# Sums over keys in an attention and MLP kernel: squares turned and added on VectorE in place of a product with ones on TensorE

## The chip, the cores and the metric

The kernel runs on one core of a Trainium2 chip. The time is the device time of one execution in microseconds. A core has five engines with a queue each, which run their instructions in order and wait for one another through semaphores: TensorE (PE in the profile; its weight loads are PEld), VectorE (DVE), ScalarE (ACT), GpSimd (POOL) and SyncE (SP, which here issues the transfers). TensorE reads SBUF and writes PSUM, which is divided into 8 banks.

## The reference

Two blocks follow each other: attention with normalised queries and keys, and an MLP without bias.

```python
batch, n_heads, seq, head_dim = (8, 12, 448, 64)
q_n, k_n = (rmsnorm(q, g_q), rmsnorm(k, g_k))
scores = scale * np.matmul(q_n, k_n.transpose(0, 1, 3, 2))
scores = scores - np.max(scores, axis=-1, keepdims=True)
attn = np.exp(scores)
attn = attn / (np.sum(attn, axis=-1, keepdims=True) + 1e-09)
attn_out = np.matmul(attn, v)
x = attn_out.transpose(0, 2, 1, 3).reshape(B * S, H * D)   # 3584 x 768
h = x @ w_in                                               # 768 x 2048
g = h - np.tanh(h)
out = g @ w_out                                            # 2048 x 768
```

All data are float32. Scores are bounded by the gains, so that the kernel leaves the maximum out (`bounded_path`; the other branch, `general_path`, isn't taken with these inputs). The sum over keys, by which each query's values are divided, is what the change is about.

## The kernel before

**Pairs and slots.** Work on attention goes by pairs of heads: 8 batches of 6 pairs, 48 pairs `s` in all. A pair's scores are held with the keys on partitions: for each of the two heads and each chunk of 128 keys (three, and a last one of 64) a matmul (L499) writes 128 keys x 448 queries into a PSUM bank and ScalarE's exponential (L504) takes it to the tile `p` in SBUF. In the last chunk the queries' halves lie on the two halves of the partitions (`p_last`). The values are products with `p` as the moving operand (L539 for the last chunk, L551 for the others); each puts 32 columns of head dimension on 32 partitions, four beside each other in the array. `divide` (L585) multiplies them by the sums' reciprocals and writes the pair's `xT`, the MLP's input.

**The sum over keys.** From the 10th pair on (`add`, L513), VectorE first adds the four chunks elementwise: L521 and L522 add the three full ones into the tile `rows` (`early["sum"]`, 128 x 2 heads x 448 queries), `add_last` (L529) adds the last, in two halves. What is left is a sum over 128 partitions. `totals` (L557) gets it from TensorE: for each half of the queries and each head a matmul (L572) of `ones` (128 x 32) with 224 columns of `rows`, four matmuls beside each other, so that 32 partitions of the bank `dn` hold the same sum. The reciprocal (L577) takes it from there to `rs`.

**The MLP** is made from seven products per group, in place of eight (the order of the products is `ORDER`, 1, 5, 6, 2, 3, 7, 4): `hidden` for a batch's first layer and `project` for its second, both by `products` (L640). Hidden: 4 groups of 7 products of 6 matmuls; output: 3 groups of 7 products of 8 matmuls; in each 168 matmuls of 224 columns. They are a generator, `stream`. Three PSUM banks named `mm` serve them in turn; products 2, 3 and 7 add to the bank of 1, 5 and 6. So product 4 takes the bank that product 2 left, and the next group's product 1 that of product 3, its product 5 that of product 7. In `hidden`, product 2 is read by a tanh (ScalarE, L676) and a subtraction (VectorE, L677); 3, 7 and 4 are added up by VectorE first (L706; L702 and L703; L710), and their tanh and a subtraction on GpSimd (L677) come when the next product is out, from the list `late["todo"]`. Factors of the second layer come from `factors` (L687 and L688 on VectorE, L689 on GpSimd) and L721. L694 (hidden) and L757, L763 (output) are ScalarE's copies out of the banks.

**The order around the change** is written by hand: `bounded_path` issues each engine's instructions in program order (`manual_schedule`), so a call's place in `slot` is its place in every engine's queue. From pair 12 on each pair has one `slot(s)`: last scores of pair s+1, last values, totals, values and division of pair s, the other scores of s+1, loads; then 56 matmuls of the stream in steps of `run(gap / 2)`, which is 7 matmuls, with other work between the steps. After 7: `add(s + 1)` and the squares; after 14: the norms of pair s+2 (`norm_blocks`, with a power on GpSimd, L457); after 21: `add_last(s + 1)`; after 28: `scale_blocks` (L464); after 35 and 42: the turning of q and k by squares of 32x32 (L474, L478); then `run(gap)`, 14 more. Pairs before the 18th have their q and k turned by TensorE instead. Six slots make a batch: the first three carry `hidden`, the other three `project`; the first slot of a batch belongs to a pair divisible by 6. Another 5 banks (`sc`, function `sc_bank`) are handed out in turn to scores, `dn` and values.

Of the kernel before, what the change touches and what calls it, by code (L numbers as in the profile page):

```python
# [9 lines left out]
F32 = mybir.dt.float32  # L10
# [3 lines left out]
ALU = mybir.AluOpType  # L14
AX = mybir.AxisListType
# [122 lines left out]
def bounded_path(tc, ctx, q, k, v, moe_w_in, moe_w_out, out, g_col, ident, ones, half_ones, neg_half, early):  # L138
# [17 lines left out]
    nc = tc.nc  # L156
    B, H, S, D = q.shape
    DFF, DM = moe_w_out.shape
    P = 128
    CP = S // NCH  # L160
    NP = H // 2
# [7 lines left out]
    HS = S // 2  # L169
# [4 lines left out]
    BL = 32  # L174
# [23 lines left out]
    def bank_of(name):  # L198

        turns[name] += 1  # L200
        return banks[name][turns[name] % len(banks[name])]
# [189 lines left out]
    normed, turned, probs, sums, whole, xT, tt = {}, {}, {}, {}, {}, {}, {}  # L391

    def squares(s):
        squares_of(nc, early["sq"], early["n"], loaded["q", s], loaded["k", s])
# [33 lines left out]
    FIRST, NJ = 3, S // BL  # L428

    def by_blocks(s):  # L430
        return has(s) and steps[s][0] >= FIRST
# [51 lines left out]
    def sc_bank():  # L483
        return bank_of("sc")

    def scores(s, c):

        rr, kT, qT = turned[s]
        halves, keys, n = (1, P, S) if c < KF else (2, KR, HS)
        name, bufs = ("p", 2) if c < 2 else ("p_full", 1) if c < KF else ("p_last", 2)  # L490
        if c == 1:
            p = probs[s, 1] = probs[s, 0]
        else:
            p = probs[s, c] = pp.tile([P, 2, 2 if c < 2 else 1, n], F32, name=name, bufs=bufs)
        tiles = [sc_bank() for _ in range(2)]
        for i in range(halves):
            for h in range(2):
                r = slice(h * D, (h + 1) * D)
                nc.tensor.matmul(  # L499
                    tiles[h][i * keys : (i + 1) * keys, :n], lhsT=kT[r, c * P : c * P + keys],  # L500
                    rhs=qT[r, i * n : (i + 1) * n], start=True, stop=True,
                )
        for h in range(2):
            nc.scalar.activation(  # L504
                p[:, h, c if c < 2 else 0, :], tiles[h][:, :n], AF.Exp,
                scale=1.0 if rr is None else rr[:, 0, 2 * c + h : 2 * c + h + 1],
            )

    def full(s):

        return probs[s, 0][:, :, 0], probs[s, 1][:, :, 1], probs[s, 2][:, :, 0]
# [12 lines left out]
    def add_last(s):  # L524
        last = probs[s, KF][:, :, 0]
        for n in range(2 if sums[s] else 0):
            t = sums[s][0]
            part = t[n * KR : (n + 1) * KR, :, n * HS : (n + 1) * HS]
            nc.vector.tensor_tensor(out=part, in0=part, in1=last[n * KR : (n + 1) * KR], op=ALU.add)  # L529

    def last_values(s, av):

        v_nat, p = loaded["v", s], probs[s, KF]
        for n in range(2):
            keys = slice(n * KR, (n + 1) * KR)
            for m in range(2):
                for h in range(2):
                    r = (2 * m + h) * BL
                    nc.tensor.matmul(  # L539
                        av[n][r : r + BL, :HS], lhsT=v_nat[keys, h, KF, m * BL : (m + 1) * BL],  # L540
                        rhs=p[keys, h, 0], start=True, stop=False,
                    )

    def values(s, av):
        v_nat, p = loaded.pop(("v", s)), full(s)
        for n in range(2):
            for c in range(KF):
                for m in range(2):
                    for h in range(2):
                        r = (2 * m + h) * BL  # L550
                        nc.tensor.matmul(  # L551
                            av[n][r : r + BL, :HS], lhsT=v_nat[:, h, c, m * BL : (m + 1) * BL],
                            rhs=p[c][:, h, n * HS : (n + 1) * HS], start=False, stop=(c == KF - 1),
                        )
        return av

    def totals(s, dn):  # L557

        parts = [t[:, h, n * HS : (n + 1) * HS] for t in sums.get(s, ()) for n in range(2) for h in range(2)]
        parts = [(parts, [ones[:, :BL]] * 2)] if parts else []  # L560
        if not sums.pop(s):
            for p in full(s):
                parts.append(
                    ([p[:, h, n * HS : (n + 1) * HS] for n in range(2) for h in range(2)], [ones[:, :BL]] * 2)
                )
            last = probs[s, KF]
            parts.append(([last[:, h, 0] for _ in range(2) for h in range(2)], [half_ones[:, n] for n in range(2)]))
        for i, (moving, by) in enumerate(parts):
            for n in range(2):
                for h in range(2):  # L570
                    r = (2 * n + h) * BL
                    nc.tensor.matmul(  # L572
                        dn[r : r + BL, :HS], lhsT=by[n], rhs=moving[2 * n + h],
                        start=(i == 0), stop=(i == len(parts) - 1),
                    )
        rs = whole[s] = sp.tile([P, HS], F32, name="rs")
        nc.vector.reciprocal(rs, dn[:, :HS])  # L577

    def divide(s, av):
        b, hp = steps[s]  # L580
        rs = whole.pop(s)
        x = xT[b, hp] = xp.tile([P, S], F32, name="xT")
        for n in range(2):
            for m in range(2):
                nc.vector.tensor_tensor(  # L585
                    out=x[m * D : (m + 1) * D, n * HS : (n + 1) * HS],
                    in0=av[n][m * D : (m + 1) * D, :HS], in1=rs[n * D : (n + 1) * D], op=ALU.mult,
                )
        for c in range(NCH):
            del probs[s, c]  # L590
        if hp < HC:
            return
        c = hp - HC
        if c == 0:
            tt[b] = tp.tile([P, 3, HC, HS], F32, name="tt", bufs=1)
        eng = nc.vector if b == 0 and c == HC - 1 else nc.gpsimd
        x11, x12, x21, x22 = (xT[b, r][:, n : n + HS] for r in (c, hp) for n in (0, HS))
        t1, t2, t4 = (tt[b][:, i, c] for i in range(3))
        eng.tensor_tensor(out=t1, in0=x12, in1=x11, op=ALU.subtract)
        eng.tensor_tensor(out=t2, in0=x22, in1=t1, op=ALU.subtract)  # L600
        eng.tensor_tensor(out=x12, in0=x22, in1=x12, op=ALU.subtract)
        eng.tensor_tensor(out=t4, in0=x21, in1=t2, op=ALU.subtract)


    late = {}
# [223 lines left out]
    def run(ns):  # L829

        spent[1] += ns
        while spent[0] + 1.0 < spent[1]:
            took = next(stream, None)
            if took is None:
                return
            spent[0] += took
# [4 lines left out]
    def gap_ns(s):  # L841

        if s < 2 * NP:
            return H_NS / 12 if s % NP < 3 else 4 * S / ENGINE_NS * CD * CF / 12
        return (H_NS + O_NS) / (4 * NP)

    def has(s):
        return 0 <= s < NS

    def first_slot(s):  # L850
# [28 lines left out]
        if has(s):  # L879
            divide(s, av)  # L880
# [31 lines left out]
    def slot(s):  # L912

        gap = gap_ns(s)
        if has(s + 1):
            scores(s + 1, KF)
        dn = sc_bank()
        av = [sc_bank() for _ in range(2)]
        last_values(s, av)
        totals(s, dn)  # L920
        divide(s, values(s, av))
        if has(s + 1):
            for c in range(KF):
                scores(s + 1, c)
        if has(s + 2):
            load(s + 2, "v")
        if by_blocks(s + 3):
            load_blocks(s + 3)
        blocks = by_blocks(s + 2)
        run(gap / 2)  # L930
        if has(s + 1):
            add(s + 1)
        if blocks:
            square_blocks(s + 2)
        run(gap / 2)
        if blocks:
            norm_blocks(s + 2)
        elif has(s + 2):
            turn(s + 2, sc_bank(), sc_bank())
        ahead = has(s + 3) and not by_blocks(s + 3)  # L940
        if ahead:
            squares(s + 3)
        if has(s + 4) and not by_blocks(s + 4):
            load(s + 4, "qk")
        run(gap / 2)
        if has(s + 1):
            add_last(s + 1)
        run(gap / 2)
        if blocks:
            scale_blocks(s + 2)  # L950
        if ahead:
            norm(s + 3)
        run(gap / 2)
        if blocks:
            turn_blocks(s + 2, 0)
        run(gap / 2)
        if blocks:
            turn_blocks(s + 2, 1)
        if ahead:
            norm_q(s + 3)  # L960
        run(gap)

    load(0, "qk")
    load(1, "qk")
# [4 lines left out]
    for s in range(NP, NS):  # L969
        (early_slot if s < 2 * NP else slot)(s)  # L970
# [346 lines left out]
```

## Time and profile before

| | |
|---|---|
| median of 9 runs (lowest to highest) | 1430.39 us (1426.14 to 1435.13) |
| profiled execution: its time, its span | 1434.06 us, 1432.2 us |
| granted TensorE clock, mean | 0.989 |
| TensorE busy (matmuls; loads) | 1397.8 us; 1176.0 us |
| VectorE busy, instructions | 867.8 us, 1396 |
| ScalarE busy, instructions | 412.2 us, 790 |
| GpSimd busy | 530.6 us |
| products with ones, of `rows` (L572) | 304 records, 38 pairs |
| reciprocal (L577), from a bank `sc` | 42, 1556 ns each |

The span reaches from the first to the last instruction of one execution. Busy times are per engine and overlap. A float32 matmul leaves two records. An instruction's line is that of the kernel's source, and a tile is named without its buffer number. "Idle before" is time in which the engine waited in front of an instruction, and the name behind the arrow is what it waited for. The chain is the sequence of work that ended last, followed back from the end.

### The profile page before, as it was taken

Reading aid. Unit: us, or ns where it says so; the run is one execution under the profiler, and the core shown is the slowest. Engines: PE = TensorE matmul, PEld = TensorE weight load, DVE = VectorE, ACT = ScalarE, POOL = GpSimd, SP = SyncE. Lnnn points to the kernel's source line nnn. Section 1 sums busy time; section 2 is a strip of 40 time slices with the busy share of each in tenths; the row PEclk is TensorE's granted clock in tenths of the full one; section 3 lists DMA queues with packets and bytes.
Section 4 is the critical chain, followed back from the end, with each engine's and each line's share of the span. In section 5 each row is a group of like instructions: output and inputs, shape, how many; then the busy total and the mean of one; then the engine's idle time right before and its main releaser. Section 6 shows DMA issues by size and latency. Waiting matters only on the chain.

```text
span 1432.2 us, 25681 instructions
## 1 busy us (share of the span) xinstructions
PE 1397.8 (98%) x10032; PEld 1176.0 (82%) x10032; DVE 867.8 (61%) x1396; ACT 412.2 (29%) x790; POOL 530.6 (37%) x348
## 2 busy tenths in 40 slices
PE   6999899999999999999999999999999999999997
PEld 3568654478998899889889988988998898899997
DVE  3899878855644676556755567545765577522311
ACT  5765454223311322122221223113221222201100
POOL 4556555232521346214533145313462145401310
PEclk9999899999999999999999999999999999999999
DMA  8669787864566656666666656666567656365663
GB/s 182 162 193 245 235 243 199 217 201 139 168 170 155 167 164 168 173 162 168 179 151 178 171 153 180 170 158 164 164 170 173 166 165 180 119 179 173 187 195 90
DMA packets 355254, 249.73 MB, mean 174 GB/s; under 512 B 266484, under 2 KB 297396, under 8 KB 355124
## 3 DMA queue, kind: packets, MB, share of 16 engines
q1 hardware_dynamic: 355120, 248.00, 64.4%
q8 instruction: 81, 1.33, 0.4%
q14 instruction: 49, 0.40, 0.1%
q10 hardware_dynamic: 4, 0.00, 0.0%
HBM read 214.50 MB, written 33.42 MB: 173 GB/s over the span
## 4 chain that ended last, share of the span: by engine, by line
PE 91%; DVE 4%; DMA 2%; SPq 1%; ACT 1%; issue 1%; POOL 0%; ACTq 0%; DVEq 0%
PE mm L640 66%; PE sc L499 9%; PE sc L551 6%; PE mm L805 4%; PE sc L572 2%; PE sc L539 2%; DMA q_nat<-in_q_dram 1%; DMA w_raw<-in_moe_w_out_dram 1%; DVE w_out L82 1%; DMA gT<-in_moe_w_in_dram 1%; DVE rs L577 1%; PE mm L551 1%; PE sc L419 0%; DVE w_out L78 0%; DVE w_out L324 0%
## 5 line engine op out<-in xcount | busy, mean ns | idle before, releaser
L640 PE MATMUL mm<-xT,w_f 128*128 128x224 f32 x1392 | 275.6, 354 | 0.0
L640 PEld LDWEIGHTS mm<-xT,w_f 128*128 128x128 f32 x1392 | 262.1, 190 | 9.1 <-issue 7.8
L640 PE MATMUL mm<-gT,w_f 128*128 128x224 f32 x1344 | 263.0, 354 | 0.0
L640 PEld LDWEIGHTS mm<-gT,w_f 128*128 128x128 f32 x1344 | 252.8, 190 | 11.4 <-issue 9.1
L457 POOL TENSOR_TENSOR rr_mine<-rr_mine,neg_half 128x28 f32<-128x28 f32 x30 | 145.1, 4835 | 256.1 <-DVE rr_mine L456 256.1
L640 PE MATMUL mm<-tt,w_f 128*128 128x224 f32 x1044 | 208.7, 353 | 0.0
L640 PEld LDWEIGHTS mm<-tt,w_f 128*128 128x128 f32 x1044 | 197.0, 190 | 3.9 <-issue 3.9
L640 PE MATMUL mm<-tg,w_f 128*128 128x224 f32 x1008 | 197.7, 353 | 0.0
L677 POOL TENSOR_TENSOR gT<-s,th 128x448 f32<-128x448 f32 x96 | 122.6, 1284 | 200.5 <-ACT th L676 197.8
L640 PEld LDWEIGHTS mm<-tg,w_f 128*128 128x128 f32 x1008 | 190.6, 190 | 0.0
L499 PE MATMUL sc<-qT,kT 64*128 64x448 f32 (+1 forms) x960 | 167.5, 497 | 12.9 <-ACT p_last L504 9.5
L499 PEld LDWEIGHTS sc<-qT,kT 64*128 64x128 f32 (+1 forms) x960 | 70.7, 166 | 84.3 <-issue 49.0
L600 POOL TENSOR_TENSOR tt<-xT,tt 128x224 f32<-128x224 f32 x23 | 17.1, 744 | 232.2 <-DVE xT L585 232.1
L676 ACT ACTIVATE th<-s 128x448 f32<-128x448 f32 x96 | 55.6, 579 | 135.3 <-DVE s L706 58.2
L577 DVE RECIPROCAL rs<-sc 128x224 f32<-128x224 f32 x42 | 65.3, 1556 | 42.6 <-PE sc L572 42.4
L504 ACT ACTIVATE p<-sc 128x448 f32<-128x448 f32 x120 | 55.6, 550 | 109.2 <-PE sc L499 109.2
L135 POOL TENSOR_TENSOR rr<-rr,neg_half 112x8 f32<-112x8 f32 (+1 forms) x36 | 59.6, 1676 | 58.5 <-DVE rr L134 58.4
L551 PE MATMUL sc<-p,v_nat 128*32 128x224 f32 x1344 | 79.1, 353 | 0.0
L805 PE MATMUL mm<-gT,w_out 128*128 128x448 f32 x192 | 76.6, 556 | 0.0
L585 DVE TENSOR_TENSOR xT<-sc,rs 64x224 f32<-64x224 f32 x168 | 65.2, 388 | 9.7 <-PE sc L551 2.3
L464 DVE TENSOR_TENSOR qk_n<-qk_nat,rr_mine 128x896 f32<-128x896 f32 x30 | 46.4, 1547 | 39.3 <-POOL rr_mine L457 37.0
L805 PEld LDWEIGHTS mm<-gT,w_out 128*128 128x128 f32 x192 | 37.0, 197 | 37.7 <-issue 36.7
(136 smaller groups left out, 1635.4 us busy)
## 6 DMA issues: line engine op xcount, KB each, us to landing
w_f<-w_in SPq DMA_DIRECT2D x196, 384.0 KB, 3.2
w_f<-w_out SPq DMA_DIRECT2D x147, 512.0 KB, 4.1
w_raw<-in_moe_w_out_dram SPq DMA_DIRECT2D x16, 768.0 KB, 5.2
out_dram<-th SPq DMA_DIRECT2D x192, 56.0 KB, 1.9
w_in<-w_out SPq DMA_DIRECT2D x21, 384.0 KB, 6.3
qk_nat<-in_q_dram SPq DMA_DIRECT2D x120, 56.0 KB, 2.5
qk_nat<-in_k_dram SPq DMA_DIRECT2D x120, 56.0 KB, 2.4
gT<-in_moe_w_in_dram SPq DMA_DIRECT2D x32, 192.0 KB, 4.2
```

Source lines behind the costliest of these rows:

```text
L135: nc.gpsimd.tensor_tensor(out=r, in0=r, in1=neg_half[:rows], op=ALU.pow)
L457: nc.gpsimd.tensor_tensor(out=mine, in0=mine, in1=neg_half[:, :1].to_broadcast([P, 2 * NJ]), op=ALU.pow)
L464: nc.vector.tensor_tensor(out=n.rearrange("p i j d -> p (i j) d"), in0=loaded.pop(("qk", s)).rearrange("p i j d -> p (i j) d"), in1=rr[:, ...
L499: nc.tensor.matmul(tiles[h][i * keys : (i + 1) * keys, :n], lhsT=kT[r, c * P : c * P + keys], rhs=qT[r, i * n : (i + 1) * n], start=True, ...
L504: nc.scalar.activation(p[:, h, c if c < 2 else 0, :], tiles[h][:, :n], AF.Exp, scale=1.0 if rr is None else rr[:, 0, 2 * c + h : 2 * c + h ...
L551: nc.tensor.matmul(av[n][r : r + BL, :HS], lhsT=v_nat[:, h, c, m * BL : (m + 1) * BL], rhs=p[c][:, h, n * HS : (n + 1) * HS], start=False, ...
L577: nc.vector.reciprocal(rs, dn[:, :HS])
L585: nc.vector.tensor_tensor(out=x[m * D : (m + 1) * D, n * HS : (n + 1) * HS], in0=av[n][m * D : (m + 1) * D, :HS], in1=rs[n * D : (n + 1) * ...
L640: nc.tensor.matmul(bank[:, f * HS : (f + 1) * HS], lhsT=w[:, c * width + f, :], rhs=moving[p](c), start=(first and f == 0 and c == 0), sto ...
L676: nc.scalar.activation(th, h, AF.Tanh, bias=0.0, scale=1.0)
L677: eng.tensor_tensor(out=g[:, rows, cols], in0=h, in1=th, op=ALU.subtract)
L805: nc.tensor.matmul(bank[:, :S], lhsT=w_out_row(f, n // HC)[:, n % HC * P : (n % HC + 1) * P], rhs=g[:, f, :], start=(f == 0), stop=(f == C ...
```

## The change

For pairs from the 14th on (`s >= 13`, `FOLDED`), the four matmuls of `totals`, the bank `dn` and the reciprocal of 128 x 224 go. In their place `fold(s + 1)` stands in the slot before, right behind `add_last(s + 1)`: VectorE turns `rows` (128 x 896) by squares of 32x32, which puts 32 queries on partitions and 32 keys side by side, and adds up each 32; what is left, 4 partial sums for each query, lies on four groups of 32 partitions. Eight ScalarE copies of 32 x 14 bring the groups side by side (64 x 4 x 14: two heads of 32 partitions). `spread_sums(s + 1)` stands in the middle of the last `run(gap)`, which is split: VectorE adds the four, takes the reciprocal of 64 x 14, copies each 32 times and turns the squares back, so that `rs_T` (64 x 448) holds each query's reciprocal on all 32 partitions of its head. `divide` reads it with one index in place of the other.

```diff
+    FOLDED = 2 * NP + 1
+
+    def fold(s):
+
+        t = sums.pop(s)[0].rearrange("p h s -> p (h s)")
+        turned_sum = late["blocks"].tile([P, 2 * S], F32, name="sum_T")
+        nc.vector.transpose(out=turned_sum, in_=t)
+        part = late["blocks"].tile([P, 2 * NJ], F32, name="sum_32")
+        nc.vector.reduce_sum(part, turned_sum.rearrange("p (i k) -> p i k", k=BL), axis=AX.X)
+        acc = whole[s] = late["blocks"].tile([2 * BL, P // BL, NJ], F32, name="sum_g")
+        for h in range(2):
+            for g in range(P // BL):
+                nc.scalar.copy(
+                    out=acc[h * BL : (h + 1) * BL, g], in_=part[g * BL : (g + 1) * BL, h * NJ : (h + 1) * NJ]
+                )
+
+    def spread_sums(s):
+
+        acc = whole[s]
+        total = late["blocks"].tile([2 * BL, NJ], F32, name="sum_all")
+        nc.vector.reduce_sum(total, acc.rearrange("p g j -> p j g"), axis=AX.X)
+        nc.vector.reciprocal(total, total)
+        wide = late["blocks"].tile([2 * BL, NJ, BL], F32, name="sum_w")
+        nc.vector.tensor_copy(out=wide, in_=total[:, :, None].to_broadcast([2 * BL, NJ, BL]))
+        rs = whole[s] = late["blocks"].tile([2 * BL, S], F32, name="rs_T")
+        nc.vector.transpose(out=rs, in_=wide.rearrange("p j k -> p (j k)"))
...
@@ divide
-                    in0=av[n][m * D : (m + 1) * D, :HS], in1=rs[n * D : (n + 1) * D], op=ALU.mult,
+                    in0=av[n][m * D : (m + 1) * D, :HS],
+                    in1=rs[:, n * HS : (n + 1) * HS] if s >= FOLDED else rs[n * D : (n + 1) * D], op=ALU.mult,
...
@@ slot
-        dn = sc_bank()
+        dn = sc_bank() if s < FOLDED else None
         av = [sc_bank() for _ in range(2)]
         last_values(s, av)
-        totals(s, dn)
+        if s < FOLDED:
+            totals(s, dn)
...
+        folded = has(s + 1) and s + 1 >= FOLDED
         if has(s + 1):
             add_last(s + 1)
+        if folded:
+            fold(s + 1)
         run(gap / 2)
...
-        run(gap)
+        run(gap / 2)
+        if folded:
+            spread_sums(s + 1)
+        run(gap / 2)
```

## The prediction

> **What bounds the kernel now.** I read the page first, for the busiest engine and for what the chain of waits is made of.
>
> ```profile
> PE 1397.8 (98%) x10032; PEld 1176.0 (82%) x10032; DVE 867.8 (61%) x1396; ACT 412.2 (29%) x790; POOL 530.6 (37%) x348
> ...
> PE 91%; DVE 4%; DMA 2%; SPq 1%; ACT 1%; issue 1%; POOL 0%; ACTq 0%; DVEq 0%
> ```
>
> TensorE sets the end: busy is no proof, but 91% of the chain is. Then the chain in order of time, for the slot of pair 24, whose products with ones are the eight records of L572 (four matmuls), and for an early slot, where the totals stand elsewhere and L551 follows L539 directly.
>
> ```profile
> 103.19 2.41 PE sc L551 x48
> ```
> ```profile
> 631.75 0.54 PE sc L499 x8
> 632.29 0.54 PE sc L539 x16
> 632.83 0.52 PE sc L572 x8
> 633.34 2.27 PE sc L551 x48
> 635.61 2.60 PE sc L499 x12
> 638.21 21.39 PE mm L640 x112
> 659.59 0.54 PE sc L499 x8
> ```
>
> Columns: start, duration, engine and line. The slot lasts 27.84 us and no other engine stands in its chain. So a microsecond less on TensorE is a microsecond gained, and a microsecond that TensorE is made to wait is lost. What can make it wait is VectorE or ScalarE holding a PSUM bank. So I read the time line of both engines behind the place where `fold` will stand, in the same slot:
>
> ```profile
> 646.35 1.26 DVE L529 TENSOR_TENSOR rows<-rows,p_last 64x448 f32<-64x448 f32 x2
> 648.10 0.62 DVE L677 TENSOR_TENSOR gT<-mm,th 128x448 f32<-128x448 f32 x1 [0.49 <-ACT th L676]
> 650.80 1.09 DVE L464 TENSOR_TENSOR qk_n<-qk_nat,rr_mine 128x896 f32<-128x896 f32 x1 [2.08 <-POOL rr_mine L457]
> ```
> ```profile
> 647.52 0.54 ACT L676 ACTIVATE th<-mm 128x448 f32<-128x448 f32 x1 [5.43 <-PE mm L640]
> ```
> ```profile
> 651.67 2.27 PEld L640 LDWEIGHTS mm<-tt,w_f 128*128 128x128 f32 x12
> ```
>
> The tanh and the subtraction L677 read the bank of the second product; the fourth (moving `tt`, loads from 651.67) needs that bank. Today it is free at 648.72, 2.9 us early. Last, the groups of instructions, for prices:
>
> ```profile
> L577 DVE RECIPROCAL rs<-sc 128x224 f32<-128x224 f32 x42 | 65.3, 1556 | 42.6 <-PE sc L572 42.4
> L504 ACT ACTIVATE p_last<-sc 128x224 f32<-128x224 f32 x60 | 18.2, 355 | 104.9 <-PE sc L499 104.9
> L452 DVE TENSOR_REDUCE rr_mine<-qk_n 128x28 f32<-128x896 f32 x30 | 32.0, 1067 | 0.0
> L454 DVE COPY rr_other<-rr_mine 32x28 f32<-32x28 f32 x120 | 24.7, 206 | 3.5
> L474 DVE STREAM_TRANSPOSE qT<-qk_n 128x448 f32<-128x448 f32 x30 | 19.2, 638 | 0.5
> L1255 ACT ACTIVATE warm<-warm 1x1 f32<-1x1 f32 x1 | 0.2, 202 | 0.0
> ```
>
> **Removed: TensorE.** With L572 between, it and L551 take 0.52 + 2.27 us; without, L551 alone takes 2.41 (the early slot). Difference 0.38. The empty 0.36 us before L572's first load are not gained: in the early slots the same gap stands before L551. By starts the removal is 633.16 - 632.76 = 0.40 (first matmuls of L551 and L572). I take 0.375 for 35 pairs (13 to 47): **-13.1 us** (14.0 by starts).
>
> **Removed: VectorE and a bank.** The reciprocal of 1.56 us goes from each slot's start, with the bank `dn`. Neither was on the chain: the first scores that need a bank back from `divide` are the fourth and fifth tiles, in both orders of the banks, and `divide` now waits only for the values. I count 0 for this; what hides it is the score matmuls, which run 1 us before those tiles.
>
> **Added: VectorE.** In `fold` a transposition of 128x896: L474 takes 0.638 for 448 columns, and 448 more at 1.0 ns (an addition, L759, takes 0.392 for 224 and L698 0.612 for 448) make 1.09, say 1.10; and a reduction like L452, 1.07. In `spread_sums` two instructions of 14 results, some 0.2 (L455, 28 columns, has 0.188) and 0.25 (with 14 reciprocals at L577's 6.9 ns), a broadcast copy of 64x448 between 0.35 and 0.62 (the 448-wide L677 is the upper end), and a transposition like L474, 0.64: about 1.6. Together 3.8 for 1.56, some 80 us more over 35 slots: VectorE goes from 868 to about 948 us, 66%, and does not become the bound. The path of `spread_sums` itself has cover: emitted 7 matmuls (2.65 us) before the slot ends, with 2.4 us of scores, last values and first values behind it before `divide` can start: 5 us for 1.6. No DMA is added or moved, SP's queue is untouched, and GpSimd gets nothing new; it only gets its inputs later.
>
> **Added: ScalarE, the step that costs.** Eight copies of 32x14 stand in ScalarE's order behind the reduction, and everything emitted after them waits: that is the tanh above. I lay this out for pair 24's slot. L529 ends at 647.61; transposition to 648.74, reduction to 649.83, eight copies to 649.86 + C, tanh 0.54 more, L677 to 651.06 + C, some 0.05 for the release. The load wants the bank at 651.67, so TensorE waits **C - 0.56 us**.
>
> For C no row is the same. The smallest instruction on ScalarE took 0.202 us (L1255). Two of L504 take 0.61 together where one takes 0.355, an overlap of 0.10: eight at a pitch of 0.11 make 0.9. Without overlap they are 1.65; VectorE's four L454 (0.206 each, 0.76 together) are close to that. The copies resemble L504 by engine and L454 by size and by changing partitions, so I take the middle, C = 1.25 (0.9 to 1.7), and a wait of 0.7 us (0.3 to 1.1).
>
> Two pages of the Trainium skill price these copies. "VectorE: DVE Perf Modes", on the errata of operands in SBUF, speaks against the change: the fixed cost is paid per instruction, many small tiles pay it each, and tiles should have 512 elements or more; its 224 + 14 cycles at 1.2 GHz give 0.198 each, 1.6 in all, which would make the wait 1.0 and the forecast about 1423. "ScalarE: Activation LUTs", on what a table load costs, lets successive instructions overlap by 93 ns, which gives 0.93, a wait of 0.4 and about 1420. The smallest row agrees with the first's single price; whether they overlap no row shows.
>
> Now the six places in a batch. **First slot** (hidden layer starts; pairs 18, 24, 30, 36, 42 show the same times within 0.4 us): 5 x 0.7 = 3.5. For pair 12, L529 ends at 310.06 and L677 would end at 313.51 + C against a load near 314.7: 0.1. **Second slot**: the tanh of the third product (today 674.20) comes after the copies. Reduction done at 677.5; L702 and L703 follow to 678.6, and the bank they free is wanted by the next group's second product at 678.76. Tanh to 678.05 + C, GpSimd's subtraction to about 680.6, L687, L688, a transposition and L696 to some 685, wanted at 685.4. Margins of 0.1 and 0.4: I put 0.15 for each of five slots, 0.75; it grows one for one when C passes 1.7. **Third slot**: L696 done at 707.7, wanted at 708.0; the next tanh is due at 708.57, as the copies end: 0. **Fourth to sixth** (output layer): fold ends about 733.1, and the next ScalarE work, L763, comes at 734.08: 0.
>
> **Sum.** -13.1 + 3.5 + 0.1 + 0.75 = **-8.8 us**. The profiled execution took 1434.06 us around a span of 1432.2, 3.7 us over the median of the runs shown; the time outside the span does not change. 1425.3 for that execution is 1421.6 against the median 1430.39: 0.6% faster.
>
> **The rivals.**
>
> *All hidden*: the copies overlap and the bank is not late; -13.1 alone, 1417.3. For it: 2.9 us of slack today. Against: the reduction alone ends 2.2 us after L529, before any copy. 0.20.
>
> *Gain mostly eaten*: C near 1.9, or VectorE's added work stretched while GpSimd runs (L464 took 1.09 in one slot, 2.01 in the next), so that the second slots wait too: 5 x 1.3 + 0.7 + 5 x 0.6 = 10.2, net -2.9, 1427.5. For it: margins of 0.1 to 0.4 us there. 0.15, a third of it within the bound of no change. The change not doing what it says, TensorE meeting another wait where the products stood, would also end near 1430; against it, the values wait for nothing in today's chain. 0.03.
>
> *Slower*: ScalarE held by the copies. At 0.4 us a copy, C = 3.2: the first slots wait 5 x 2.65, pair 12 2.0, the second slots 5 x 1.65, together 23.5; net +10, 1440. It decides from C = 2.35, 0.29 us a copy. For it: the in-order queue, and that each copy changes partitions. Against: no ScalarE row of any size costs more than 0.20 fixed. 0.10.
>
> **How the numbers follow.** Forecast 0.52, all hidden 0.20, mostly eaten 0.15, no effect 0.03, slower 0.10. This kernel's measurement tells 0.2% (2.9 us) from no change. Faster: 0.52 + 0.20 + 0.10 = 0.82; within: 0.05 + 0.03 = 0.08; slower 0.10. The range: low 1415, all hidden with 0.40 us a pair and a microsecond or so of scatter between runs; high 1429, where the first slots wait 1.7 each and the second 0.8. Outside it are the slower case and part of no effect.
>
> **What would show it.** Right: 24 records of L572 on `rows` in place of 304, slots of the output layer 0.38 us shorter (27.46), the first slots of a batch longer than those, with a wait of a load at L640 for VectorE's L677 at the fourth product; eight ScalarE copies in 0.9 to 1.7 us; VectorE near 948 us. Wrong: waits of TensorE in second or third slots above 0.5 us, `divide` waiting for the transposition of `spread_sums`, or a gap beyond 0.36 us ahead of the values.

## The result and the profile after

| | before | changed |
|---|---|---|
| median | 1431.06 us (31 runs) | 1425.24 us (10 runs, 1422.94 to 1429.03) |
| ratio of the changed to before | | 0.9962, 95% interval 0.9952 to 0.9973 |
| profiled execution: time, span | 1434.06 us, 1432.2 us | 1420.67 us, 1418.9 us |
| span from pair 12's last values (first load of L539) to the end | 1137.95 us | 1131.55 us |

The change makes the kernel 0.4% faster, 5.8 us by the medians. The spans of the two profiled executions differ by 13.3 us, but 6.9 of these lie ahead of pair 12's last values, in code that the change leaves as it is: that place was reached between 287.4 and 294.3 us in the executions profiled for this study. The last row leaves this part out: 6.4 us. I use it below for all kernels.

The page after, engines and chain, answers to the first lines of before:

```profile
PE 1382.5 (97%) x9752; PEld 1162.6 (82%) x9752; DVE 928.2 (65%) x1571; ACT 467.1 (33%) x1070; POOL 524.5 (37%) x348
...
PE 87%; DVE 4%; DMA 3%; SPq 2%; ACT 2%; issue 1%; POOL 0%; ACTq 0%; DVEq 0%
```

TensorE has 280 records less, VectorE 60 us more work and ScalarE 55 more, and still TensorE is 87% of the chain. The chain in order of time over four slots (pairs 23 to 26; columns are start, duration, engine and line; L551 opens each slot's values):

```profile
596.47 2.41 PE sc L551 x48
...
623.93 2.41 PE sc L551 x48
626.34 2.60 PE sc L499 x12
628.94 4.75 PE mm L669 x24
...
652.67 2.41 PE sc L551 x48
...
680.13 2.41 PE sc L551 x48
```

From start to start a slot takes 27.46 us where it was 27.84, except for the first slot of the batch (from 623.93): 28.74. There the chain leaves the products (L669, line 640 before) after 24 records, which are twelve matmuls. The time lines of VectorE, ScalarE and the weight loads in that slot:

```profile
637.09 1.26 DVE L529 TENSOR_TENSOR rows<-rows,p_last 64x448 f32<-64x448 f32 x2
638.38 1.11 DVE L586 STREAM_TRANSPOSE sum_T<-rows 128x896 f32<-128x896 f32 x1
639.53 1.09 DVE L588 TENSOR_REDUCE sum<-sum_T 128x28 f32<-128x896 f32 x1
643.08 0.62 DVE L706 TENSOR_TENSOR gT<-mm,th 128x448 f32<-128x448 f32 x1 [2.46 <-ACT th L705]
```
```profile
640.71 1.77 ACT L592 COPY sum_g<-sum 32x14 f32<-32x14 f32 x8 [7.89 <-DVE sum L588]
642.50 0.54 ACT L705 ACTIVATE th<-mm 128x448 f32<-128x448 f32 x1
```
```profile
643.75 2.19 PEld L669 LDWEIGHTS mm<-tt,w_f 128*128 128x128 f32 x12 [1.35 <-DVE gT L706]
```

The tanh starts 0.02 us after the last copy, the subtraction (L706, before L677) ends at 643.70 and the fourth product's load starts at 643.75, after 1.35 us of waiting. Loads ahead of it end at 642.40, so this is where it was wanted. VectorE itself was idle for 2.46 us ahead of L706: it waited for ScalarE.

### The profile page after: what moved, and what is told of

Read it like the earlier page. It is cut to its first block, busy times and chain, and to the rows that moved or that the text cites. A ratio compares the mean times of both kernels' runs of the same rounds, so it can differ in the third digit from the quotient of the medians.

```text
span 1418.9 us, 25566 instructions
## 1 busy us (share of the span) xinstructions
PE 1382.5 (97%) x9752; PEld 1162.6 (82%) x9752; DVE 928.2 (65%) x1571; ACT 467.1 (33%) x1070; POOL 524.5 (37%) x348
## 4 chain that ended last, share of the span: by engine, by line
PE 87%; DVE 4%; DMA 3%; SPq 2%; ACT 2%; issue 1%; POOL 0%; ACTq 0%; DVEq 0%
PE mm L669 64%; PE sc L499 9%; PE sc L551 7%; PE mm L834 4%; PE sc L539 2%; DMA w_f<-w_in 1%; SPq L118 1%; SPq L265 1%; DMA w_raw<-in_moe_w_out_dram 1%; DVE w_out L82 1%; PE mm L551 1%; DMA gT<-in_moe_w_in_dram 1%; ACT sum_g L592 0%; DVE rs L577 0%; SPq L116 0%
## 5 line engine op out<-in xcount | busy, mean ns | idle before, releaser
L669 PE MATMUL mm<-xT,w_f 128*128 128x224 f32 x1392 | 275.6, 354 | 0.0
L669 PEld LDWEIGHTS mm<-xT,w_f 128*128 128x128 f32 x1392 | 262.1, 190 | 9.1 <-issue 7.2
L669 PE MATMUL mm<-gT,w_f 128*128 128x224 f32 x1344 | 263.0, 354 | 0.0
L669 PEld LDWEIGHTS mm<-gT,w_f 128*128 128x128 f32 x1344 | 252.8, 190 | 11.4 <-issue 6.5
L669 PE MATMUL mm<-tt,w_f 128*128 128x224 f32 x1044 | 209.4, 354 | 5.4 <-DVE gT L706 5.4
L669 PEld LDWEIGHTS mm<-tt,w_f 128*128 128x128 f32 x1044 | 196.5, 190 | 11.4 <-DVE gT L706 7.5
L669 PE MATMUL mm<-tg,w_f 128*128 128x224 f32 x1008 | 197.7, 352 | 0.0
L706 POOL TENSOR_TENSOR gT<-s,th 128x448 f32<-128x448 f32 x96 | 115.6, 1214 | 212.8 <-ACT th L705 212.7
L669 PEld LDWEIGHTS mm<-tg,w_f 128*128 128x128 f32 x1008 | 190.6, 190 | 0.0
L592 ACT COPY sum_g<-sum 32x14 f32<-32x14 f32 x280 | 56.3, 201 | 225.1 <-DVE sum L588 219.4
L613 DVE TENSOR_TENSOR xT<-sc,rs_T 64x224 f32<-64x224 f32 x140 | 54.4, 388 | 68.3 <-PE sc L551 66.4
L504 ACT ACTIVATE p<-sc 128x448 f32<-128x448 f32 x120 | 55.5, 548 | 97.8 <-PE sc L499 97.8
L551 PE MATMUL sc<-p,v_nat 128*32 128x224 f32 x1344 | 79.9, 355 | 0.0
L521 DVE TENSOR_TENSOR rows<-p 128x896 f32<-128x896 f32 x38 | 42.4, 1115 | 41.7 <-ACT p L504 41.7
```

What stands on the lines that cost most here:

```text
L504: nc.scalar.activation(p[:, h, c if c < 2 else 0, :], tiles[h][:, :n], AF.Exp, scale=1.0 if rr is None else rr[:, 0, 2 * c + h : 2 * c + h ...
L521: nc.vector.tensor_tensor(out=t, in0=p[0], in1=p[1], op=ALU.add)
L551: nc.tensor.matmul(av[n][r : r + BL, :HS], lhsT=v_nat[:, h, c, m * BL : (m + 1) * BL], rhs=p[c][:, h, n * HS : (n + 1) * HS], start=False, ...
L592: nc.scalar.copy(out=acc[h * BL : (h + 1) * BL, g], in_=part[g * BL : (g + 1) * BL, h * NJ : (h + 1) * NJ])
L613: nc.vector.tensor_tensor(out=x[m * D : (m + 1) * D, n * HS : (n + 1) * HS], in0=av[n][m * D : (m + 1) * D, :HS], in1=rs[:, n * HS : (n + ...
L669: nc.tensor.matmul(bank[:, f * HS : (f + 1) * HS], lhsT=w[:, c * width + f, :], rhs=moving[p](c), start=(first and f == 0 and c == 0), sto ...
```

## The experiments

Each kernel is the changed one with the edit shown. "From pair 12" is the span from pair 12's last values to the end (before 1137.95, changed 1131.55).

**1. The copies issued later.**

```diff
+    def gather(s):
+        part = late.pop("part")
         acc = whole[s] = late["blocks"].tile(...)
         ... the eight copies, out of fold ...
@@ slot, after 35 matmuls
         run(gap / 2)
+        if folded:
+            gather(s + 1)
         if blocks:
             turn_blocks(s + 2, 0)
```

> The same instructions as in the changed kernel; only the eight ScalarE copies are issued 14 matmuls later in each slot, ahead of the turning of q. Theory (13.1 us come from TensorE, and about 7 are lost because the first slots' tanh waits in ScalarE's queue behind copies that wait for VectorE): the tanh starts as the product ends, L706 ends about 641.3 in the slot where its bank is wanted at 642.4, no wait is left: 1418 us against 1431 before, ratio 0.991. Rival A (the loss comes from VectorE's own order, the transposition and the reduction standing ahead of the subtraction): first slots still 1.3 us longer, 1425. Rival B (the removed products are worth only 6 us and nothing is lost): 1425.

> The kernel with the copies issued 14 matmuls later once more, for a narrower interval: 1418 us, ratio 0.991 to 0.992.

Measured: 1418.52 against 1429.29 us, ratio 0.9922 (0.9895 to 0.9949), and 1415.02 against 1428.88 us in the longer comparison, 0.9901 (0.9882 to 0.9920). From pair 12: 1124.15 and 1123.90, 14 us less than before. The same instructions in the first slot of the batch, ScalarE and then VectorE:

```profile
641.98 0.54 ACT L710 ACTIVATE th<-mm 128x448 f32<-128x448 f32 x1 [5.43 <-PE mm L674]
644.43 1.77 ACT L597 COPY sum_g<-sum 32x14 f32<-32x14 f32 x8 [1.91 <-DVE sum L588]
```
```profile
643.26 1.09 DVE L588 TENSOR_REDUCE sum<-sum_T 128x28 f32<-128x896 f32 x1
644.26 0.61 DVE L711 TENSOR_TENSOR gT<-mm,th 128x448 f32<-128x448 f32 x1
```
```profile
646.13 2.27 PEld L674 LDWEIGHTS mm<-tt,w_f 128*128 128x128 f32 x12
```

The tanh is done by 642.52, the subtraction waits only for VectorE's reduction and ends at 644.87; the load at 646.13 has no idle time ahead of it. VectorE's order was unchanged, so rival A falls; the gain more than doubled, so rival B falls. This version beats both kernels.

**2. The copies on VectorE, at their old place.**

```diff
-                nc.scalar.copy(
+                nc.vector.tensor_copy(
```

> The eight copies are made by VectorE at the same place, behind the reduction. Theory: ScalarE is free, the tanh is done early, but the subtraction now waits behind eight copies of 0.19 us on VectorE: it ends about 642.7 where the bank is wanted at 642.4, a wait of 0.3 to 0.4 us in five slots: 1420 us, ratio 0.992. Rival A: the wait grows with what VectorE does there, to 2.8 us, 1433. Rival B: 1425, as the copies' engine does not matter.

Measured: 1461.48 us, ratio 1.0228 (1.0209 to 1.0246); from pair 12 1169.12, 31 us more than before. The theory and both rivals missed this. The first slot behaved as the theory said: from start to start 27.84, 0.38 of waiting. The second and third slots of the batch were the surprise, in the chain:

```profile
630.49 2.41 PE sc L551 x48
...
658.33 2.41 PE sc L551 x48
...
688.12 2.41 PE sc L551 x48
...
721.13 2.41 PE sc L551 x48
```

They take 29.79 and 33.01 us, 2.3 and 5.5 more than 27.46. In two of the five batches (pairs 31 and 43) the second slot takes 31.5, which experiment 5 comes back to. VectorE's time line gives the copies of the three slots, and the loads' time line the waits:

```profile
647.19 1.51 DVE L592 COPY sum_g<-sum 32x14 f32<-32x14 f32 x8
674.84 2.37 DVE L592 COPY sum_g<-sum 32x14 f32<-32x14 f32 x8
706.45 4.13 DVE L592 COPY sum_g<-sum 32x14 f32<-32x14 f32 x8
```
```profile
678.45 4.46 PEld L669 LDWEIGHTS mm<-tt,w_f 128*128 128x128 f32 x24 [2.41 <-DVE s L732]
711.29 6.14 PEld L669 LDWEIGHTS mm<-xT,w_f 128*128 128x128 f32 x24 [3.94 <-DVE s L725]
```

The evictions L732 and L725, queued behind the copies, release the banks that the next products want; these were the places for which the prediction had found margins of 0.1 and 0.3 us. And the copies are not the same everywhere: 0.19 us each in the first slot, 0.52 in the third, where GpSimd's 128x448 subtractions run from 706.85 to 710.16. That GpSimd is the cause was not tested. What else the third slot lost is told under experiment 5.

**3. The removal alone.**

```diff
     def fold(s):
+        sums.pop(s)
+        if s == FOLDED:
+            late["one"] = late["blocks"].tile([2 * BL, S], F32, name="rs_T")
+            nc.vector.memset(late["one"], 1.0)
+        whole[s] = late["one"]
+        return
...
     def spread_sums(s):
+        return
```

> The products with ones, the bank and the reciprocal are left out from the 14th pair on and nothing takes their place: the division reads a tile of ones, so the sums over keys of these pairs are not part of the result. Theory: all slots of the output layer and of the hidden layer are 27.46 us, 35 times 0.375 us less than before: 1418, ratio 0.991. Rival A: the same. Rival B: 1425, since that is all the products were worth.

Measured: 1416.44 us, ratio 0.9921 (0.9897 to 0.9944); from pair 12 1124.13, 13.8 less than before. All slots in its chain are 27.46 us from pair 17 on, where before has 27.84, and 28.39 for pairs 13 to 15, where before has 28.77. So TensorE's part of the change is worth 13.8 us, and the version of experiment 1, which does all the work, costs no more than this one, which does none of it.

**4. The added work alone.**

```diff
-        t = sums.pop(s)[0].rearrange("p h s -> p (h s)")
+        t = sums[s][0].rearrange("p h s -> p (h s)")
...
-        dn = sc_bank() if s < FOLDED else None
+        dn = sc_bank()
...
-        if s < FOLDED:
-            totals(s, dn)
+        totals(s, dn)
...  divide reads rs as before
```

> The products with ones and the reciprocal stay and are used; the turning, adding, the eight ScalarE copies and the spreading are done as in the changed kernel, their result unused. Theory: the added work alone costs five first slots 1.28 us each and pair 12's slot 0.6: 7.0 us, 1438 against 1431, ratio 1.005; VectorE also has the reciprocal, which ends before this. Rival A: the same 7. Rival B: 1431, nothing lost.

Measured: 1439.29 against 1429.29 us, ratio 1.0079 (1.0055 to 1.0102), so 10 us, and by the interval no less than 7.9; from pair 12 1146.23, 8.3 more than before. In the chain the first slots take 29.09 us (630.06 to 659.15) where 27.84 is the rule, the others from pair 17 on 27.84 to 27.88. That accounts for 1.25 in five slots, some 6.3 us. The slots of pairs 12 and 13 lost 2.2 together (from 288.59 to 348.38, 59.79 us, where before has 57.58) and not 0.6: besides a wait of 0.74 us for the subtraction in pair 12's slot, the score loads of pair 13's wait for the reciprocal.

```profile
321.79 0.29 PEld L499 LDWEIGHTS sc<-qT,kT 64*128 64x128 f32 x2 [1.23 <-DVE rs L577]
```

VectorE's queue was late there: one instruction (L404, the scaling of queries), just ahead, took 4.18 us where it took 0.77 at this place before, and the work of `spread_sums` followed. So "VectorE also has the reciprocal, which ends before this" was wrong in this one slot; the rest agrees with the theory.

**5. Every copy made twice.**

```diff
+        for twice in range(2):
             for h in range(2):
                 for g in range(P // BL):
                     nc.scalar.copy(
```

> All eight copies are made twice, so ScalarE is held 1.77 us longer in each of 34 slots. Theory (the wait is what ScalarE's queue holds back, less a margin): the five first slots wait 1.28 + 1.77 each, pair 12's 0.6 + 1.77, and the second slots, which today end within some 0.1 us of their margin, 1.7 each: 15.2 + 2.4 + 8.5 = 26 lost against 13.1 gained, 1444 us, ratio 1.009. Rival C (only the first slots are near their margin, the second ones are not): 1435.

Measured: 1449.68 us, ratio 1.0135 (1.0110 to 1.0159); from pair 12 1160.11, 22 more than before and 36 more than experiment 3, where 26 had been expected. The second slots lost 1.5 each (666.76 to 695.71, 28.95), where the theory had 1.7; rival C falls. TensorE waits there 0.76 us for ScalarE's own copy out of a bank (L724, L694 before) and 0.89 for the addition L726 (L696 before). The first slot of pair 24 took 31.95 us (634.81 to 666.76), 4.5 over the rule and not 3.05; the other four took 32.05 to 33.60. The loads' time line, and the group of the matmuls behind them (the number after the busy time is the mean in ns):

```profile
656.44 3.60 PEld L670 LDWEIGHTS mm<-tt,w_f 128*128 128x128 f32 x12 [3.16 <-DVE gT L707]
```
```profile
L670 PE MATMUL mm<-tt,w_f 128*128 128x224 f32 x12 | 3.9, 505 | 2.8 <-DVE gT L707 2.8
```

The wait of 3.16 us is the expected one. But the twelve loads behind it take 3.60 us where they take 2.19 in the changed kernel, and their matmuls 505 ns where 354 is the mean. The granted clock by stages says why (busy times of PE, PEld, DVE, ACT and POOL with their counts, then the clock, the share of the DMA engines and GB/s):

```profile
656.40:660.10 3.70, 3.65 (x12) 3.41 (x13) 3.11 (x5) 1.16 (x2) 1.43 (x2) 0.60 0.01 2
660.10:663.00 2.90, 2.90 (x17) 2.90 (x16) 2.45 (x5) 1.36 (x3) 0.95 (x2) 1.00 0.40 136
```

After 2.8 us without a matmul TensorE ran at 0.60 of its clock for 3.7 us: another 1.4 us lost. In experiment 2 the third slot shows the same: 3.94 us of waiting, and loads of 6.14 us where 24 take 4.54 in an undisturbed slot. Its second slot waited 2.41 us (2.1 without a matmul) and the 24 loads behind took 4.46: nothing lost. But the second slots are not alike. With the same wait, the loads of pair 31's took 6.14, and the granted clock, 1.00 behind the wait in pair 19's, was 0.63 in pair 31's:

```profile
851.48 6.14 PEld L669 LDWEIGHTS mm<-tt,w_f 128*128 128x128 f32 x24 [2.40 <-DVE s L732]
```
```profile
505.60:510.00 4.40, 4.34 (x23) 4.34 (x24) 4.19 (x5) 1.15 (x3) 3.42 (x3) 1.00 0.25 57
851.40:856.00 4.60, 4.51 (x15) 4.19 (x16) 4.39 (x6) 1.17 (x3) 3.60 (x3) 0.63 0.09 36
```

Pair 43's is like pair 31's, and these are the two that took 31.5 us. So 2.1 us without a matmul cost 1.7 in two slots of five and nothing in three, and 2.8 us cost between 1.4 and 3.1 in the five first slots of experiment 5: the length of the gap does not settle it alone, and what else does is open. The Trainium skill has such a rule in "TensorE: Matmul & The Clock Gate", Part 1, on the HAM clock gate: the clock is halved after an idle window of about 3.4 us. Gaps of 2.8 us, and some of 2.1, are shorter than that, and the clock fell all the same.

**6. The copies without change of partitions.**

```diff
-                    ..., in_=part[g * BL : (g + 1) * BL, h * NJ : (h + 1) * NJ]
+                    ..., in_=part[h * BL : (h + 1) * BL, h * NJ : (h + 1) * NJ]
```

> The eight copies read the partitions that they write, so that none changes partitions; the sums over keys of the folded pairs are wrong in it, the work is the same. Theory D (0.224 us from copy to copy, no overlap, comes from changing partitions): the pitch falls to about 0.11, the eight take 1.0 us, the first slots wait 0.5 each: 1421 us. Theory E (0.224 is what any so small ScalarE instruction takes): eight take 1.77 us as before and the time stays 1425.

Measured: 1418.66 us, ratio 0.9926 (0.9906 to 0.9947); from pair 12 1127.07. Its copies in a first slot, ScalarE's time line:

```profile
641.23 1.05 ACT L592 COPY sum_g<-sum 32x14 f32<-32x14 f32 x8 [7.88 <-DVE sum L588]
```

1.05 us in place of 1.77 at the same duration of one (198 and 201 ns): the pitch falls from 0.22 to 0.12. Theory D holds, E falls. The first slot is 28.01 us (624.46 to 652.47), a wait of 0.55. In the chain four copies that start on the same partitions overlap by 0.1; the one at which the group of partitions changes does not. In the changed kernel the four copies of a head write the same partitions and only those that they read change, and none of its copies overlap; so it needs no change of those written. What a change of those written alone would do was not tested.

**7. Two copies in place of eight.**

```diff
-        for h in range(2):
-            for g in range(P // BL):
-                nc.scalar.copy(...)
+        flat = acc.rearrange("p g j -> p (g j)")
+        for i in range(2):
+            nc.scalar.copy(out=flat[:, i * 2 * NJ : (i + 1) * 2 * NJ], in_=part[: 2 * BL])
```

> Two copies of 64x28 at the same place instead of eight of 32x14; the partial sums of the upper 64 partitions are left out of the sums. ScalarE still waits there for VectorE's reduction, but holds its queue only some 0.45 us after it. Theory: the tanh starts 0.45 us after the reduction, its bank is free about when it is wanted, no wait over 0.1 us: 1418 us, ratio 0.991. Rival F (it is the waiting for the reduction, not the copies' length, that costs): the first slots keep about 1 us, 1424.

Measured: 1416.87 us, ratio 0.9914 (0.9893 to 0.9934); from pair 12 1123.86. The two copies take 0.33 us, and in the first slot L704, the subtraction, ends at 640.74:

```profile
638.14 1.09 DVE L588 TENSOR_REDUCE sum<-sum_T 128x28 f32<-128x896 f32 x1
640.12 0.62 DVE L704 TENSOR_TENSOR gT<-mm,th 128x448 f32<-128x448 f32 x1 [0.89 <-ACT th L703]
```

All slots in its chain are 27.46 us from pair 17 on. ScalarE still waits for the reduction here, and TensorE loses nothing: that waiting uses up most of the margin, and it is the copies' length that passes it. Rival F falls.

Together, experiments 7, 6, the changed kernel and 5 make a series in the time C that the copies hold ScalarE: C = 0.33, 1.05, 1.77 and 3.58, and the loss of pair 24's slot 0, 0.55, 1.28 and 4.5, of which 1.4 came with the clock. Without the clock that is C - 0.5, from the margin on.

## Why the prediction was right or wrong

**TensorE, -13.1 us: right.** The step read from the early slots (L551 alone 2.41 against 0.52 + 2.27) gave 0.375 a pair; the slots became 0.38 shorter, which makes 13.3 for 35 pairs; experiment 3 gave 13.8, and the other 0.5 lies at the end, behind the last products, where the profile of before has 8.2 us and that of experiment 3 7.6. The empty 0.36 us ahead of L572 did move to L551, as assumed:

```profile
623.86 0.54 PEld L551 LDWEIGHTS sc<-p,v_nat 128*32 128x32 f32 x16 [0.36 <-issue]
```

**VectorE's added work: right; its busy time and one wait: not.** In groups of the changed kernel (the number after the busy time is the mean in ns), the parts of `spread_sums`:

```profile
L605 DVE STREAM_TRANSPOSE rs_T<-sum_w 64x448 f32<-64x448 f32 x35 | 22.3, 637 | 1.2
L603 DVE COPY sum_w<-sum_all 64x448 f32<-64x448 f32 x35 | 16.1, 461 | 1.2
L601 DVE RECIPROCAL sum_all<-sum_all 64x14 f32<-64x14 f32 x35 | 8.1, 232 | 1.2
L600 DVE TENSOR_REDUCE sum_all<-sum_g 64x14 f32<-64x56 f32 x35 | 7.9, 227 | 0.0
```

They sum to 1.56 us against 1.6, and the transposition of 896 columns with its reduction to 2.2 against 2.17. With 131.3 us of new rows and 54.4 of reciprocals gone, the net is 77 us where some 80 were forecast. The sign "VectorE near 948 us" did not come all the same: it was busy for 928, since other rows became shorter (L464 41.1 us in place of 46.4, L521 42.4 in place of 44.8) or overlapped more.

`divide` (L613) found VectorE idle ahead of it for 68.3 us in all, 66.4 of them waiting for the values (L551), so `rs_T` was in time as a rule. In pair 13's slot it was not: L404 held VectorE for 4.18 us, `spread_sums` came late, `divide` started right behind it and the scores waited for their bank:

```profile
321.72 0.30 PEld L499 LDWEIGHTS sc<-qT,kT 64*128 64x128 f32 x4 [0.53 <-DVE xT L613]
```

That slot took 28.64 us where experiment 3 has 28.39. It is the one place where the cover of 5 us, counted for the path of `spread_sums`, was not there.

**The copies, "the step that costs": the mechanism and the place were right, the size too small.** C was put at 1.25, the middle between overlapping (0.9) and not (1.65); it was 1.77, outside its own range (0.9 to 1.7), because copies that change partitions do not overlap at all, and stand 0.02 apart besides. The row that the working had called similar for just this reason, L454, showed four in 0.76, and eight at that pitch are 1.5; going to the middle meant giving L504, which stays on its partitions, half the weight. With 1.77 in "C - 0.56" the wait is 1.21 against 1.28 measured. For five first slots: 6.4 in place of 3.5. Pair 12's slot lost 0.6 in place of 0.1, the same C.

**The second slots, 0.75: nothing was lost.** At 1.77 they lost none (27.46 us), but L725, the former L696, ended at 677.06, within about 0.1 us of where its load was wanted. "It grows one for one when C passes 1.7" came near: at 3.58 that makes 1.9, and they lost 1.5. The price was too high, the threshold about right. One of the two waits there, that for ScalarE's own copy L694, was not in the working.

**Sum.** With the measured terms 35 x 0.38 = 13.3 less 6.4 (five first slots), 0.6 (pair 12's) and 0.25 (pair 13's) is 6.0 us; the end behind the last products was 0.4 shorter besides, and the span from pair 12 shows 6.4, the medians 5.8; forecast were 8.8 (1421.6 us). The term mis-sized is the wait for the copies: 7.0 in all, forecast 3.6; the 0.75 of the second slots, which did not come, made up for part of it by luck. The result lies between the forecast and the rival "gain mostly eaten", which had C = 1.9 and waits in the second slots; C was near that, the waits were not there. The rival "slower" had its point at 0.29 us a copy; it did turn slower when the copies were doubled, and further than worked out, since it did not count the loss of clock.

**The two page rules.** The Trainium skill's "VectorE: DVE Perf Modes", on the errata of operands in SBUF, gave an estimate of 0.198 us for one copy and 1.6 for eight, and was the nearer one (0.201 and 1.77 measured). Its "ScalarE: Activation LUTs", on what a table load costs, has successive instructions overlap by about 93 ns; that agrees with the copies of experiment 6 (0.198 each, 1.05 for eight) but not with those whose partitions change.

## To carry to other kernels

Work that is moved off the bounding engine is free only if nothing behind it in the queue it lands in frees a buffer of that engine too late: look in each kind of slot for the next instruction in that queue and for its margin, not at the queue's busy share (ScalarE was 33% busy). Where an instruction has to wait for another engine, issue it after the ones that don't, as late as its own reader allows: 14 matmuls later turned a gain of 0.4% into one of 0.8 to 1.0%. Price a run of small instructions by a row with the same change of partitions, and test the margin by making the added piece longer and shorter.

## What was not expected of the hardware

- ScalarE's copies of 32x14 overlap by 0.1 us if they stay on their partitions (eight in 1.05 us) and not at all in the changed kernel, where the partitions read change from each to the next (1.77 us).
- VectorE's copies of 32x14 took 0.19 us each beside a GpSimd that ran a power of 28 columns, and 0.52 beside GpSimd subtractions of 128x448; that GpSimd made the difference was not tested.
- After 2.8 us without a matmul TensorE's granted clock was 0.60 for the next 3.7 us, and a wait of 3.16 us cost 4.5; after 2.1 us the clock fell in two slots of five (0.63 for 4.6 us in pair 31's) and stayed at 1.00 in the others.
